# A chunked attention recurrence before two expert layers: other shapes for its small matmuls, one product for two uses, and a fixed order of the first transfers

## The chip, the cores and the metric

The kernel runs on one core of a Trainium2 chip. Its engines work from queues of their own: TensorE (PE for the matmuls, PEld for the loads of their weights), VectorE (DVE), ScalarE (ACT), GpSimd (POOL), and SyncE (SP), which issues nearly all DMAs here. The metric is the time of one execution on the device in microseconds (us), as the median of several. The profiled execution gives the rows.

## The reference

Three stages follow each other. The change is in the first and in the router of the second.

```python
# attention: B, H, S, D = 4, 8, 768, 40; the state is D x D for each (batch, head)
for t in range(S):
    y[:, :, t] = einsum('bhd,bhde->bhe', r_t, state)
    Sa = einsum('bhde,bhe->bhd', state, a_t)
    state = state * w_t[:, :, None, :] - einsum('bhd,bhe->bhde', Sa, b_t) + einsum('bhd,bhe->bhde', v_t, k_t)
x = y as (3072 tokens, 320)
# experts: skip = x @ w_skip > 0; the expert is argmax(x @ w_gate) of 8
x[skip] += gate * (relu(x @ w1[e]) @ w2[e])        # 320 -> 1024 -> 320
# dense layer, 320 -> 2048 -> 320
h = x @ w_in;  out = (h * sigmoid(1.702 * h)) @ w_out
```

## The kernel before, in words

The 768 steps are cut into 12 chunks of 64; all 32 (batch, head) pairs of a chunk are worked on together, packed in halves of 64 partitions. Everything in the recurrence is fp32, and an fp32 matmul stands as two instructions in the trace (a transpose as one).

For a chunk, `g_load` brings the decays (`wt`), the a vectors (`at`) and the k and b vectors (`kbT`). `g_prep` forms running products of the decays with two scans on VectorE (L216, L229) and their inverses. `g_a` (L265) and `g_kb` (L279) scale `at` and `kbT` by them on GpSimd; `g_f` and `g_kb` turn tiles with PE transposes (L251, L292). Three products of keys and a vectors follow. `g_gram` takes the 32-wide diagonal blocks that must be inverted (L320: 64 small matmuls for a chunk, with weights of 32 columns). `g_ag`, once for each of two parities, takes the whole 64 x 64 product (L378: 32 matmuls with 64x64 weights), which VectorE masks into `m0`, `m1` (L383). For each pair of chunks, VectorE inverts the blocks: a transpose (L330), 62 operations that depend on each other (L343, L346), a transpose back (L351), and DMAs from `Tc` into `tz` (L360), four for a chunk.

The serial part of a chunk is `g_chain`: sums X (L422 from the values, L427 from the state), the inverse times X (L444), a correction (L453), the inverse again, copies to `vu`. `g_state` (L483, L487) and `g_sn` (L509) make the next state. `g_vt`, `g_pq` (L554) and `g_post` (L578, L582) form the output rows, 64 matmuls on the keys and the state for a chunk, and `put` and `logits` (L827, L837) store them and form the router's sums with fp32 transposes and matmuls.

Between the products stand warm matmuls (L601) that compute nothing of use and keep TensorE active: `g_burst` adds 18 twice in a chunk, and `g_warm` adds more whenever the counted activity falls behind `PACE` times the elapsed time.

The order on every engine is fixed when the program is built. Each piece of work is a Python generator that yields what it needs and a cost, such as `'P1.05*.40'` (engine, us, counted activity); `weave` advances the one that can start first by these costs, and near-ties go by due times, the numbers in `RANK`. Each engine's queue then runs in that order, waiting on semaphores. SBUF of the later stages is opened when the last chunk is through its chain (`moves`).

Of the kernel before, what the change touches and what calls it, by code (L numbers as in the profile page):

```python
# [23 lines left out]
def host_attn(r, k, v, w, a, b):  # L24
    B, H_, S, D_ = r.shape
    NC = S // L

    def five(z):
        return z.reshape(2, 2, H, NC, L, D)

    k5, b5, v5, r5 = five(k), five(b), five(v), five(r)
    ch = lambda z: z.transpose(3, 0, 5, 2, 1, 4)
    kb = np.stack([ch(k5), ch(b5)], 5)
    kb[:, 1] = kb[:, 1, :, :, :, ::-1].copy()
    w5 = ch(five(w))
    wz = np.zeros((2, NC, 2, D, H, 2, L), np.float32)
    for h in (0, 32):
        wz[0][..., h + 1:h + 32] = w5[..., h:h + 31]
        wz[1][..., h:h + 31] = w5[..., h + 1:h + 32]
    pairs = lambda z: z.reshape(2, 2, H // 2, 2, NC, L, D).transpose(4, 3, 6, 0, 1, 2, 5).reshape(NC, 2, D, 1024)  # L40
    c = np.ascontiguousarray
    return dict(at=c(ch(five(a))).reshape(NC, 2, D, 1024), kbT=c(kb).reshape(NC, 2, D, 2048),
                rT=c(np.stack([pairs(r5), pairs(v5)], 3)).reshape(NC, 2, D, 2048),
                rv=np.pad(v5.transpose(3, 0, 4, 1, 2, 5), [(0, 0)] * 5 + [(0, 24)]).reshape(NC, 2, L, 1024), wt=c(wz.transpose(1, 2, 3, 0, 4, 5, 6)).reshape(NC, 2, D, 2048))
# [63 lines left out]
class Attn(Flow):  # L108
# [12 lines left out]
    EARLY = 'wt at0 at1 at2 kbT0 kbT1 W c_d1 c_d2 Za Z Tc tmp x y m0 m1 tz'.split()  # L121

    def __init__(self, tc, ctx, args, NC, emit_x):
# [14 lines left out]
        nc.vector.memset(self.wt, 1.0)  # L138
        for q, i in ((0, 0), (1, 31)):
            nc.vector.memset(self.wt[:, q].rearrange('p (a s) -> p a s', s=32)[:, :, i:i + 1], 0.0)  # L140
        for n, d in (('c_32', F32), ('c_16', F16)):
            shp = args[n].shape
            t = self.cst.tile([128, shp[1]], d, name=n)
            nc.sync.dma_start(out=t, in_=args[n])
# [6 lines left out]
        for n, i in (('c_d1', 0), ('c_d2', 31)):  # L151
            t = self.C[n] = new([128, 1024], F32, n)
            nc.gpsimd.memset(t, 0.0)
            nc.gpsimd.memset(t.rearrange('p (a s) -> p a s', s=32)[:, :, i:i + 1], 1.0)
        self.at = [new([128, 8, 2, 64], F32, f'at{i}') for i in range(3)]
        self.kbT = [new([128, 8, 2, 128], F32, f'kbT{i}') for i in range(2)]
        self.rT = [new([128, 2, 16, 64], F32, f'rT{i}') for i in range(2)]
        for t in self.at + self.kbT:
            nc.gpsimd.memset(t, 0.0)
        self.tz = new([128, 16, 64], F32, 'tz')  # L160
        self.tot = self.cst.tile([128, NC, 16, 2], F32, name='tots')
        self.scl = self.cst.tile([128, NC, 16], F32, name='scl')
        self.begin(self.SLOTS)
        self.ST = [new([128, 16, 64], F32, f'ST{i}') for i in range(2)]
        self.vu = [new([128, 32, 64], F32, f'vu{i}') for i in range(2)]
        for t in self.ST + self.vu:
            nc.gpsimd.memset(t, 0.0)
        self.S = self.tile([128, 8, 128], F32, 'S')
        nc.gpsimd.memset(self.S, 0.0)
        self.x, self.y = (self.tile([128, 664], F32, z) for z in 'xy')  # L170
        self.km = [self.tile([128, 1304], F32, f'km{i}') for i in range(self.KM)]
        for t in (self.x, self.y, *self.km):
            nc.gpsimd.memset(t[:, -24:], 0.0)
        self.zrow = self.ST[0][0:1].rearrange('p a b -> p (a b)')[:, :320].bitcast(F16)

# [6 lines left out]
    def g_zero(self):  # L182
        yield f'D1.1'
        self.nc.vector.memset(self.tz, 0.0)
        self.mark('zero', 0)

    def g_load(self, c):

        for n, need, t, cost in (('wt', ('W', c - 1), self.wt.rearrange('p a b -> p (a b)'), 1.6),
                                 ('at', ('X', c - 3), self.at[c % 3].rearrange('p a b c -> p (a b c)'), .8),  # L190
                                 ('kbT', ('km', c - 2), self.kbT[c % 2].rearrange('p a b c -> p (a b c)'), 1.6)):
            yield need
            if n == 'at':
                yield ('ag', c - 3)
            if n == 'kbT':
                yield ('ag', c - 2)
            for hb in range(2):
                yield f'Q.6>E{cost}'
                self.nc.sync.dma_start(out=t[64 * hb:64 * hb + 40], in_=self.args[n][c, hb])
            self.mark('l' + n, c)  # L200

    def g_prep(self, c):

        yield ('lwt', c)
        nc, s = self.nc, self.ch[c]
        wt = self.wt
        C1, C2 = self.C['c_d1'], self.C['c_d2']
        seg = lambda z: z.rearrange('p (a s) -> p a s', s=32)
        rv = slice(None, None, -1)
        yield ('F', c - 2)  # L210
        yield ('as', c - 2)
        yield ('kb', c - 2)
        yield 'D2.35'
        W = self.tile([128, 2, 1024], F32, 'W', 2)
        wf, wb = W[:, 0], W[:, 1]
        nc.vector.tensor_tensor_scan(out=wf, data0=wt[:, 0], data1=C1, initial=0.0, op0=ALU.mult, op1=ALU.add)  # L216
        yield 'D.2'
# [3 lines left out]
        yield 'D.36'  # L221
        tot = self.tile([128, 32, 1], F32, 'tot')
        nc.vector.reciprocal(out=tot, in_=full)
        yield 'D.15|G1.06'
        nc.vector.tensor_copy(out=seg(C2)[:, 1::2, 31:32], in_=tot[:, 1::2])
        f1 = seg(wf)[:, 0::2]
        nc.gpsimd.tensor_tensor(out=f1, in0=f1, in1=tot[:, 0::2].to_broadcast([128, 16, 32]), op=ALU.mult)
        yield 'D2.35'
# [3 lines left out]
        if c:  # L232
            yield 'D.5'
            nc.vector.tensor_tensor(out=self.scl[:, c - 1].rearrange('p (r h) -> p h r', r=2),
                                    in0=self.tot[:, c - 1, :, 1].rearrange('p (h r) -> p h r', r=2),
                                    in1=self.tot[:, c, :, 0].rearrange('p (h r) -> p h r', r=2), op=ALU.mult)
            self.mark('scl', c - 1)

    def g_f(self, c):

        yield ('W', c)
        nc, s = self.nc, self.ch[c]
        yield ('xo', 2 * c - 7)
        F = self.tile([128, 2, 8, 40], F32, 'F', 4)
        for q in range(2):
            yield '+g'
            sg = self.got
            yield 'P.45*.23'
            ps = self.pst(sg)
            for h in range(4):  # L250
                nc.tensor.transpose(out=ps[:, 128 * h:128 * h + 128], in_=s['W'][:, 0, 512 * q + 128 * h:512 * q + 128 * h + 128], identity=self.C['c_id'])  # L251
# [7 lines left out]
    def g_a(self, c):  # L259
# [5 lines left out]
        self.nc.gpsimd.tensor_tensor(out=t, in0=t, in1=self.ch[c]['W'][:, 0], op=ALU.mult)  # L265
        self.mark('as', c)

    def g_kb(self, c):
# [4 lines left out]
        W = s['W'][:, 1].rearrange('p (a b t) -> p a b t', b=2, t=64)  # L273
        kbT = self.kbT[c % 2]
        for q in range(2):
            yield 'G2.4'
            t = kbT[:, 4 * q:4 * q + 4].rearrange('p a b (e t) -> p (a b) e t', e=2)
            w = W[:, 4 * q:4 * q + 4].rearrange('p a b t -> p (a b) t').unsqueeze(2).to_broadcast([128, 8, 2, 64])
            nc.gpsimd.tensor_tensor(out=t, in0=t, in1=w, op=ALU.mult)  # L279
        self.mark('kb', c)  # L280
        yield ('Y', c - self.KM)
        km = self.km[c % self.KM]
        s['km'] = km
        km = km[:, :1280].rearrange('p (b q h d) -> p b q h d', b=2, q=2, d=40)
        for q in range(2):
            for par in range(2):
                yield '+g'
                sg = self.got
                yield 'P.45*.23'
# [9 lines left out]
    def g_gram(self, c0):  # L299
# [3 lines left out]
        yield ('zt', c0 - 2)  # L303
        Za = self.tile([128, 2, 2, 256], F32, 'Za')
        for i, c in enumerate(pair):
            yield ('as', c)
            yield ('kb', c)
            at, kbT = self.at[c % 3], self.kbT[c % 2]
            yield '+g2'
            sg = self.got  # L310
            yield 'P1.2*.41'
            Ad = [self.pst(z) for z in sg]
            for h in range(8):
                for par in range(2):
                    for half in range(2):
                        q = 64 * par + 32 * half
                        for hb in range(2):
                            r = slice(64 * hb, 64 * hb + 64)
                            o = 64 - 64 * hb + 32 * half
                            mm(Ad[hb][q:q + 32, 32 * h:32 * h + 32], lhsT=kbT[r, h, par, o:o + 32],  # L320
                               rhs=at[r, h, par, 32 * half:32 * half + 32], start=True, stop=True)
            self.mark('Ad', c)
            for hb in range(2):
                yield 'A.37'
                nc.scalar.copy(out=Za[:, i, hb], in_=Ad[hb][:, :256])
                self.give(sg[hb])
# [6 lines left out]
        yield 'P.43*.49'  # L333
# [14 lines left out]
        yield ('te', c0 - 3)  # L348
        Tc = self.tile([128, 2, 512], F32, 'Tc', 2)
# [5 lines left out]
        for i, c in enumerate(pair):  # L355
            yield ('U', c - 1)
            yield 'Q2.4>E1.2'
            for q in range(4):
                sl = slice(32 * q, 32 * q + 32)
                nc.sync.dma_start(out=tz[sl, :, q % 2 * 32:q % 2 * 32 + 32], in_=Tc[sl, i].rearrange('p (u t) -> p u t', t=32))  # L360
            self.mark('te', c)

    def g_ag(self, c, par):

        yield ('Ad', c)
        nc, s = self.nc, self.ch[c]
        at, kbT = self.at[c % 3], self.kbT[c % 2]
        yield ('B', c - 2)
        yield '+g2'
        sg = self.got  # L370
        yield 'P1.05*.54'
        ps = [self.pst(z) for z in sg]
        for h in range(8):
            for q in range(2):
                for hb in range(2):
                    r = slice(64 * hb, 64 * hb + 64)
# [3 lines left out]
        m = s[f'm{par}'] = self.tile([128, 2, 8, 64], F32, f'm{par}', 2)  # L380
        for hb in range(2):
            yield 'D.69'
# [1145 lines left out]
```

## Time and profile before

| | |
|---|---|
| median of 3 runs | 1057.68 us (1053.57 to 1057.70) |
| the profiled execution | 1056.17 us, of which 1054.3 us lie between the first and the last instruction |
| TensorE busy, matmuls / weight loads | 899.8 us / 700.3 us |
| VectorE, ScalarE, GpSimd busy | 575.9, 357.2, 372.6 us |
| mean granted TensorE clock | 0.923 of full |

Three stretches are told apart below by the time from the first instruction. Up to 114 us the first pair of chunks is loaded and inverted, until its first product with the inverse starts. The twelve chains then run to 515 us, and from there the expert stage runs to 705 us and the dense layer to the end. An engine that is busy is not therefore the bound; matmuls overlap, and the durations of PE rows are modelled, so that the time that a train of them takes is read from the chain of work.

### The profile page before, as it was taken

The page shows a single profiled execution, that of the slowest core. Times are in us where ns is not written, and L with a number is a line of the kernel's source. Part 1 is how long each engine was busy: PE and PEld are TensorE (multiplying, and loading weights), DVE is VectorE, ACT ScalarE, POOL GpSimd, SP SyncE. Part 2 cuts the span into 40 slices and gives each one's busy share as a digit, 9 for nine tenths or more (in the row PEclk, how much of TensorE's full clock was granted, in tenths as well). Part 3 has the DMA queues.
Part 4 walks back from the last instruction along what each step waited for, and adds up shares of the span by engine and source line. Part 5 has one row for each costly group of instructions (what it writes and reads, how often), then busy time and mean ns, then how long its engine had stood idle before and what let it go on. Part 6 is the DMA issues. An engine that isn't in the chain of part 4 may idle for free.

```text
span 1054.3 us, 36252 instructions
## 1 busy us (share of the span) xinstructions
PE 899.8 (85%) x16428; PEld 700.3 (66%) x16428; DVE 575.9 (55%) x1080; ACT 357.2 (34%) x708; POOL 372.6 (35%) x283
## 2 busy tenths in 40 slices
PE   5778798979998898899921889868799999999998
PEld 5768677879888788788811768753345555555565
DVE  2449577458768577383475888676972222122110
ACT  0110231323242233233344556634543333333330
POOL 5460312413532332411225367443543333333220
PEclk9889798989999999899855989988999999999999
DMA  5531243433344234123357976714301010100000
GB/s 128 137 86 28 47 119 74 112 100 105 96 119 111 69 116 121 34 73 74 114 176 227 256 206 201 247 31 123 85 27 39 13 38 13 39 14 13 13 20 28
DMA packets 81959, 96.86 MB, mean 92 GB/s; under 512 B 58740, under 2 KB 68728, under 8 KB 76856
## 3 DMA queue, kind: packets, MB, share of 16 engines
q1 hardware_dynamic: 79496, 90.12, 31.0%
q0 software_dynamic: 2304, 4.36, 1.5%
q8 instruction: 131, 2.15, 0.9%
q14 instruction: 28, 0.23, 0.1%
HBM read 70.70 MB, written 14.48 MB: 81 GB/s over the span
## 4 chain that ended last, share of the span: by engine, by line
PE 61%; DVE 13%; issue 11%; DMA 7%; ACT 3%; POOL 2%; SPq 2%; DVEq 0%; ACTq 0%; POOLq 0%
PE gx L601 8%; PE g L1352 5%; PE c L1392 5%; PE c L1393 5%; PE c L1391 5%; PE g L1354 3%; PE g L578 3%; PE g L444 3%; PE gx L1352 2%; PE g L554 2%; PE g L378 2%; PE g L487 2%; PE g L292 2%; PE g L483 1%; DMA kbT<-kbT 1%
## 5 line engine op out<-in xcount | busy, mean ns | idle before, releaser
L1374 POOL TENSOR_TENSOR glo<-g,ghi 128x512 f16<-128x512 f32 x96 | 114.8, 1198 | 200.3 <-ACT ghi L1373 200.1
L601 PE MATMUL gx<-c 128*128 128x128 f16 x2073 | 147.6, 227 | 11.8 <-issue 4.5
L601 PEld LDWEIGHTS <-c 128*128 128x128 f16 x2073 | 130.7, 102 | 19.1 <-issue 9.4
L1370 DVE SCALAR_TENSOR_TENSOR g<-g,sg 128x512 f32<-128x512 f32 x64 | 43.9, 688 | 135.9 <-ACT sg L1368 135.9
L1392 PE MATMUL c<-wo_lo,ghi 128*128 128x320 f16 x384 | 114.8, 299 | 1.9 <-DVE wo_lo L1299 1.9
L1391 PE MATMUL c<-wo_hi,ghi 128*128 128x320 f16 x384 | 114.8, 299 | 0.7 <-ACT wo_hi L1296 0.7
L1393 PE MATMUL c<-wo_hi,glo 128*128 128x320 f16 x384 | 115.0, 299 | 0.0
L1352 PE MATMUL g<-xt,wi_hi 128*128 128x512 f16 x320 | 81.7, 387 | 18.6 <-DMA xt<-xe 12.7
L1352 PEld LDWEIGHTS <-wi_hi 128*128 128x128 f16 x480 | 47.5, 99 | 65.3 <-DMA xt<-xe 13.0
L1373 ACT CAST ghi<-g 128x512 f16<-128x512 f32 x96 | 59.2, 618 | 79.3 <-DVE g L1370 78.5
L805 POOL TENSOR_TENSOR xr<-xo,xr 128x256 f16<-128x256 f32 (+1 forms) x44 | 21.2, 502 | 169.4 <-ACT xr L801 169.3
L279 POOL TENSOR_TENSOR kbT<-kbT,W 128x1024 f32<-128x1024 f32 x24 | 60.8, 2553 | 40.3 <-DMA kbT<-kbT 37.8
L343 DVE TENSOR_TENSOR tmp<-tm,Z 128x31 f32<-128x31 f32 (+15 forms) x186 | 63.3, 340 | 9.9 <-PE tm L336 4.1
L346 DVE TENSOR_TENSOR tm<-tm,tmp 128x31 f32<-128x31 f32 (+15 forms) x186 | 64.8, 349 | 5.9
L1368 ACT ACTIVATE sg<-g 128x512 f32<-128x512 f32 x64 | 37.8, 595 | 66.6 <-PE g L1354 66.6
L383 DVE TENSOR_TENSOR m<-g,c 128x512 f32<-128x512 f32 x48 | 31.1, 681 | 51.7 <-PE g L378 51.7
L1370 DVE SCALAR_TENSOR_TENSOR g<-gx,sg 128x512 f32<-128x512 f32 x32 | 22.1, 689 | 63.7 <-ACT sg L1368 63.4
L1038 POOL TENSOR_TENSOR w2l<-w2s,w2h 128x1280 f16<-128x1280 f32 x16 | 44.9, 2813 | 28.5 <-ACT w2h L1036 26.8
L1103 PE MATMUL g<-g_xt,w1h 128*128 128x240 f16 x220 | 31.5, 275 | 25.5 <-DMA g_xt<-g_x 25.4
L1354 PE MATMUL g<-xt,wi_lo 128*128 128x512 f16 x192 | 53.1, 386 | 0.0
L1392 PEld LDWEIGHTS <-ghi 128*128 128x128 f16 x384 | 37.6, 98 | 21.6 <-issue 1.0
L1354 PEld LDWEIGHTS <-wi_lo 128*128 128x128 f16 x288 | 28.5, 99 | 34.9 <-issue 1.6
(170 smaller groups left out, 1902.5 us busy)
## 6 DMA issues: line engine op xcount, KB each, us to landing
w2s<-w SPq DMA_DIRECT2D x8, 1280.0 KB
w1s<-w1a SPq DMA_DIRECT2D x8, 1024.0 KB
wt<-wt SPq DMA_DIRECT2D x24, 320.0 KB
rT<-rT SPq DMA_DIRECT2D x24, 320.0 KB
kbT<-kbT SPq DMA_DIRECT2D x24, 320.0 KB
vu<-rv SPq DMA_DIRECT2D x24, 256.0 KB
d_s<-wo SPq DMA_DIRECT2D x10, 512.0 KB
d_s<-wia SPq DMA_DIRECT2D x8, 512.0 KB
```

The costliest lines, as they stand in the source:

```text
L279: nc.gpsimd.tensor_tensor(out=t, in0=t, in1=w, op=ALU.mult)
L343: nc.vector.tensor_tensor(out=tv, in0=Tm[:, st:, st:st + 1].to_broadcast([128, n, st]), in1=Z[:, st:st + 1, 0:st].to_broadcast([128, n, st ...
L346: nc.vector.tensor_tensor(out=Tm[:, st:, 0:st], in0=Tm[:, st:, 0:st], in1=tv, op=ALU.subtract)
L601: self.nc.tensor.matmul(self.X[:, 384:], lhsT=self.C['c_i'], rhs=self.C['c_tm'][:, :128], start=self.first, stop=True, skip_group_check=True)
L1352: nc.tensor.matmul(h, lhsT=self.whi[:, k % 3, fs], rhs=xt[:, k], start=k == 0, stop=False)
L1354: nc.tensor.matmul(h, lhsT=self.wlo[:, k, fs], rhs=xt[:, k], start=False, stop=k == 2)
L1370: nc.vector.scalar_tensor_tensor(out=g, in0=h, scalar=2.0 ** -6, in1=sg2, op0=ALU.mult, op1=ALU.mult)
L1373: nc.scalar.copy(out=ghi[:, f], in_=g)
L1374: nc.gpsimd.tensor_tensor(out=glo[:, f], in0=g, in1=ghi[:, f], op=ALU.subtract)
L1391: nc.tensor.matmul(o, lhsT=ghi[:, f, s], rhs=self.ohi[:, f], start=f == 0, stop=False)
L1392: nc.tensor.matmul(o, lhsT=ghi[:, f, s], rhs=self.olo[:, f], start=False, stop=False)
L1393: nc.tensor.matmul(o, lhsT=glo[:, f, s], rhs=self.ohi[:, f], start=False, stop=f == 15)
```

## The change

Part by part, in the order of the diff (cut; the table `RANK` has new numbers throughout, and the costs that the pieces yield are new too):

- Loads: decays come once, unshifted, into `w5`, and ScalarE makes the two shifted copies (`g_split`). Transfers have 48 rows for each half in place of 40. The memsets become pieces of work (`sets`), and a counter `iss` fixes the order of the first transfers: wt, at, identity, kbT of chunk 0; wt, at, kbT of chunk 1; values; the rest. Constants of the router come after.
- `g_prep`: the reciprocal is split in two, the product of totals goes to GpSimd. For the first two chunks `kbT` is scaled on VectorE.
- The small product of `g_gram` goes. `g_ag` takes 16 matmuls with 64x128 weights for a parity, and both the mask (VectorE) and the diagonal blocks (eight ScalarE copies for a chunk) are read from its result.
- `tz` is filled by eight DMAs for a chunk. The inverse times X streams 40 columns in place of 64, as does the product that makes the state. The first chunk's products with the zero state go.
- `S` holds two heads block-diagonally; `g_post` runs for each half: 16 matmuls with the keys (40 columns) and 8 with the state (80 columns), in place of 32 and 32 for both halves.
- Router sums: 5 fp16 transposes and 8 fp16 matmuls on the high and low halves, in place of 3 and 3 in fp32.
- Warm matmuls: `PACE` .45 in place of .6 (.6 until the first chain), in groups of 6; the activity that the pieces are counted with is mostly larger. `weave` counts TensorE instructions and allows 3.75 us for each 128.

```diff
+        yield 'D', .97, ('z5', 0), lambda: D(self.w5, 1.0)
...
+        i = dict(wt=(1, 5), at=(2, 6), kbT=(4, 7))[n][c] if c < 2 else 10
+        if i > 1:
+            yield ('iss', i - 1)
+        yield f'Q.4>E{cost}|Q.4>E{cost}'
+        for hb in range(2):
+            self.nc.sync.dma_start(out=t[64 * hb:64 * hb + 48], in_=self.args[n][c, hb])
...
+        for q in range(2):
+            yield 'A1.1'
+            self.nc.scalar.copy(out=seg(self.wt[:, q])[:, :, 1 - q:32 - q], in_=seg(self.w5)[:, :, q:q + 31])
...
-            yield 'G2.4'
+            yield 'G2.4' if c > 1 else 'D1.15'
...
-                            mm(Ad[hb][q:q + 32, 32 * h:32 * h + 32], lhsT=kbT[r, h, par, o:o + 32],
-                               rhs=at[r, h, par, 32 * half:32 * half + 32], start=True, stop=True)
...
-        yield ('te', c0 - 3)
-        Tc = self.tile([128, 2, 512], F32, 'Tc', 2)
+        yield ('te', c0 - 1)
+        Tc = self.tile([128, 2, 512], F32, 'Tc')
...
-        yield ('B', c - 2)
+        yield ('zt', c - c % 2 - 2)
+        yield ('B', c - 3)
...
-        yield 'P1.05*.54'
+        yield 'P1.9*1.05*e*32'
         ps = [self.pst(z) for z in sg]
         for h in range(8):
-            for q in range(2):
-                for hb in range(2):
-                    r = slice(64 * hb, 64 * hb + 64)
-                    o = slice(64 * (q ^ hb), 64 * (q ^ hb) + 64)
-                    nc.tensor.matmul(ps[hb][o, 64 * h:64 * h + 64], lhsT=kbT[r, h, par, o], rhs=at[r, h, par], start=True, stop=True)
+            for hb in range(2):
+                r = slice(64 * hb, 64 * hb + 64)
+                nc.tensor.matmul(ps[hb][:, 64 * h:64 * h + 64], lhsT=kbT[r, h, par], rhs=at[r, h, par], start=True, stop=True)
...
+            for half in range(2):
+                o = 64 - 64 * hb + 32 * half
+                nc.scalar.copy(out=Za[o:o + 32, c % 2, par].rearrange('p (h t) -> p h t', t=32), in_=p3[o:o + 32, :, 32 * half:32 * half + 32])
...
-                mm(U[par][u, 64 * h:64 * h + 64], lhsT=tz[o, 8 * hb + h], rhs=x[o, 320 * hb + 40 * h:320 * hb + 40 * h + 64], start=h == 0, stop=True, **kw)
+                mm(U[par][u, 40 * h:40 * h + 40], lhsT=tz[o, 8 * hb + h], rhs=x[o, 320 * hb + 40 * h:320 * hb + 40 * h + 40], start=True, stop=True)
...
-                    mm(ps[64 * hb:64 * hb + 40, 64 * h:64 * h + 64], lhsT=km[:, p], rhs=vu[:, p], start=False, stop=True, **kw)
+                    mm(ps[64 * hb:64 * hb + 40, 64 * h:64 * h + 40], lhsT=km[:, p], rhs=vu[:, p, :40], start=False, stop=True, **kw)
...
+        for j in range(4):
+            for e in range(2):
+                for par in range(2):
+                    mm(Y[64 * par:64 * par + 64, 80 * j + 40 * e:80 * j + 40 * e + 40], lhsT=pq[:, 4 * par + j, e], rhs=km[:, hb, par, 2 * j + e],
+                       start=j + e == 0, stop=not c, **kw)
...
+            for j in range(4):
+                for par in range(2):
+                    mm(Y[64 * par:64 * par + 64, 80 * j:80 * j + 80], lhsT=rT[:, 8 * hb + 4 * par + j],
+                       rhs=S[:, 4 * par + j, hb].rearrange('p e d -> p (e d)'), start=False, stop=True, **kw)
...
-    PACE, SURPLUS = .6, .1
+    PACE, SURPLUS, FIRST = .45, .3, .6
...
+                    while page + n >= PAGE:
+                        t, cost, n, page = max(t + cost * (PAGE - page) / n, came), cost - cost * (PAGE - page) / n, n - (PAGE - page), 0
+                        came = t + FETCH
...
-            nc.tensor.transpose(out=ps[:n, 128 * k:128 * k + 128], in_=x[:, 128 * k:128 * k + n], identity=A.C['c_id'])
+            nc.tensor.transpose(out=p16[:, 128 * k:128 * k + 128], in_=xr[:, 128 * k:128 * k + 128], identity=A.C['c_i'])
```

## Rows read from the trace of the kernel before

**Rows 1.** Busy us (count) of PE, PEld, DVE, ACT, POOL; clock, DMA share, GB/s.

```profile
0.00:30.00 30.00, 15.88 (x219) 15.65 (x220) 9.00 (x9) 1.71 (x2) 15.94 (x24) 0.87 0.59 128
...
110.00:515.00 405.00, 366.46 (x11637) 328.49 (x11639) 256.03 (x547) 118.82 (x318) 121.14 (x97) 0.94 0.34 89
```

**Rows 2.** Chain of waits, shares by line: 0 to 110, then 110 to 515.

```profile
by line: issue 34.9%; DMA kbT<-kbT 14.1%; DMA wt<-wt 7.8%; POOL kbT L279 7.0%; DVE W L229 4.9%; PE g L378 3.3%; POOL vu L167 3.2%; POOL kbT L159 3.2%; POOL at L159 2.4%; DVE W L216 2.1%; SPq L782 1.8%; SPq L199 1.8%; POOL c_d L153 1.7%; POO
...
by line: PE gx L601 19.5%; issue 9.3%; PE g L578 7.3%; PE g L444 7.1%; PE g L554 6.0%; PE g L487 5.6%; PE g L378 4.9%; PE g L292 4.0%; PE g L483 3.8%; PE g L582 3.3%; PE g L320 3.3%; PE g L837 3.3%; PE gx L453 3.3%; PE gx L427 3.2%; PE gx L
```

**Rows 3.** Timeline up to the first product with the inverse: start, us, what.

```profile
14.90 0.51 SPq L199 DMA_DIRECT2D wt<-wt  x1
23.62 2.29 DVE L216 TENSOR_TENSOR_SCAN W<-wt,c_d 128x1024 f32<-128x1024 f32 x1 [19.33 <-DMA wt<-wt]
43.70 5.32 POOL L279 TENSOR_TENSOR kbT<-kbT,W 128x1024 f32<-128x1024 f32 x2 [1.28 <-DMA kbT<-kbT]
73.47 2.00 DVE L330 STREAM_TRANSPOSE Z<-Za 128x1024 f32<-128x1024 f32 x1 [6.05 <-ACT Za L325]
105.50 1.87 DVE L351 STREAM_TRANSPOSE Tc<-tm 128x1024 f32<-128x1024 f32 x1
107.39 2.77 SPq L360 DMA_DIRECT2D tz<-Tc  x4
114.17 1.99 PE L444 MATMUL g<-x,tz 64*64 64x64 f32 x64
```

**Rows 4.** Groups of VectorE instructions, 110 to 515 us.

```profile
L343 DVE TENSOR_TENSOR tmp<-tm,Z 128x31 f32<-128x31 f32 (+15 forms) x155 | 52.7, 340 | 6.9 <-PE tm L336 2.1
L383 DVE TENSOR_TENSOR m<-g,c 128x512 f32<-128x512 f32 x40 | 25.9, 681 | 40.5 <-PE g L378 40.5
```

**Rows 5.** Chain of work, pieces between 178 and 262 us: start, us, what.

```profile
180.97 2.12 PE gx L601 x36
...
185.25 0.72 PE g L837 x6
185.96 1.09 PE g L378 x64
187.05 0.48 PE g L827 x3
...
207.31 1.02 PE g L487 x32
...
234.07 0.64 PE g L530 x16
...
244.72 2.02 PE g L578 x64
246.74 1.09 PE g L582 x64
...
255.64 1.22 PE g L320 x79
```

**Rows 6.** Timeline of PEld around one stop, 168 to 174 us.

```profile
168.59 1.03 PEld L320 LDWEIGHTS g<-at,kbT 64*32 64x32 f32 x110
173.23 0.28 PEld L320 LDWEIGHTS g<-at,kbT 64*32 64x32 f32 x18 [3.60 <-issue]
```

**Rows 7.** Instruction queue: 170.4 to 172.4 us, 110 to 515, 346.5 to 361.

```profile
q8 instruction: 1, 0.02, 3.7%
...
q8 instruction: 91, 1.49, 1.6%
...
q8 instruction: 5, 0.08, 2.3%
```

**Rows 8.** Busy time: dense stretch, two stops; L601 alone, 110 to 515.

```profile
346.50:361.00 14.50, 12.49 (x546) 10.65 (x545) 6.18 (x10) 5.25 (x14) 4.93 (x3) 1.00 0.23 47
...
211.00:219.00 8.00, 3.45 (x145) 3.11 (x132) 3.96 (x3) 1.30 (x4) 0.00 (x0) 0.79 0.45 117
...
110.00:515.00 405.00, 95.14 (x1293) 80.25 (x1292) 0.94 0.34 89
```

More of the change, by code (lines that the diff above doesn't have):

```diff
@@ L137, in __init__ @@
         self.wt = new([128, 2, 1024], F32, 'wt')
-        nc.vector.memset(self.wt, 1.0)
-        for q, i in ((0, 0), (1, 31)):
-            nc.vector.memset(self.wt[:, q].rearrange('p (a s) -> p a s', s=32)[:, :, i:i + 1], 0.0)
+        self.w5 = new([128, 1024], F32, 'w5')
+        self.cin = []
         for n, d in (('c_32', F32), ('c_16', F16)):
@@ L176, in tile, with g_set, g_const @@
+    def g_set(self, eng, cost, what, fn):
+        yield f'{eng}{cost}'
+        fn()
+        self.mark(*what)
+    def g_const(self, i):
+        n, t = self.cin[i]
+        yield ('iss', 2 if i == 0 else 8)
+        yield 'Q.4>E1.0' if i == 0 else 'Q.4>E1.8'
+        self.nc.sync.dma_start(out=t, in_=self.args[n])
+        self.mark(n, 0)
+        self.note('iss', 3 if i == 0 else 9)
     def tile(self, shape, dt, name, bufs=1):
@@ L302, in g_gram @@
         pair = range(c0, c0 + 2)
[L303 to L317, printed above, removed]
-                            r = slice(64 * hb, 64 * hb + 64)
-                            o = 64 - 64 * hb + 32 * half
-                            mm(Ad[hb][q:q + 32, 32 * h:32 * h + 32], lhsT=kbT[r, h, par, o:o + 32],
-                               rhs=at[r, h, par, 32 * half:32 * half + 32], start=True, stop=True)
[L322 to L326, printed above, removed]
+        for c in pair:
+            yield ('ag', c)
+        Za = self.zas[c0 // 2]
         yield ('elim', c0 - 2)
@@ L356, in g_gram @@
             yield ('U', c - 1)
[L357 to L360, printed above, removed]
+            yield 'Q3.2>E1.2'
+            for q in range(8):
+                hb, half, par = 1 - q // 4, q // 2 % 2, q % 2
+                sl, o = slice(32 * (q // 2), 32 * (q // 2) + 32), 64 * par + 32 * half
+                nc.sync.dma_start(out=tz[o:o + 32, 8 * hb:8 * hb + 8, 32 * half:32 * half + 32],
+                                  in_=Tc[sl, i, 256 * par:256 * par + 256].rearrange('p (u t) -> p u t', t=32))
@@ new lines, in g_ag @@
+        if c // 2 not in self.zas:
+            self.zas[c // 2] = self.tile([128, 2, 2, 256], F32, 'Za')
+        Za = self.zas[c // 2]
+        m = s[f'm{par}'] = self.tile([128, 2, 8, 64], F32, f'm{par}', 3)
+        for hb in range(2):
+            yield 'D.69|A.36|A.36'
+            p3 = ps[hb].rearrange('p (h t) -> p h t', t=64)
+            nc.vector.tensor_tensor(out=m[:, hb], in0=p3, in1=self.two[:, hb:hb + 1].to_broadcast([128, 8, 64]), op=ALU.mult)
+            for half in range(2):
+                o = 64 - 64 * hb + 32 * half
+                nc.scalar.copy(out=Za[o:o + 32, c % 2, par].rearrange('p (h t) -> p h t', t=32), in_=p3[o:o + 32, :, 32 * half:32 * half + 32])
+            self.give(sg[hb])
@@ L408, in g_chain @@
         yield ('gram', c)
+        yield ('warm', 0)
         yield ('v', c)
         yield ('zero', 0)
+        yield ('zx', 0)
+        yield ('zs', 0)
         yield ('D', c - 1)
@@ L612, in g_warm @@
     def g_warm(self):
+        yield ('c_16', 0)
         yield 'Z1'
```

392 lines of the change are left out of this document (214 added, 178 removed), and 50 rows, old and new, of the table RANK.

## The prediction, made before the changed kernel ran

> **What bounds the kernel now.** I read the busy time by stretch first [rows 1]. From 110 to 515 us TensorE is the busiest engine (weight loads 328 of 405 us, VectorE 256). The change touches the two later stages, after 515 us, through the order of work alone. The chain of waits tells the two early stretches apart [rows 2]: up to 110 us it holds transfers, memsets, GpSimd and a long "issue" piece, while from 110 to 515 us nearly all of it is PE lines and PE's own "issue" (9.3%, 38 us). So in the chains PE's queue is the bound, and the largest single line in it, L601 (19.5%), computes nothing of use.
>
> The timeline of the start shows what is late [rows 3]: the second half of the first decays is issued only at 14.90 us, behind transfers that are not needed yet in SP's fixed order, and the scan starts at 23.62. The keys of chunk 0 are scaled at 43.70, the pair's blocks come to VectorE at 73.47, the inverse leaves at 105.50, and its first product starts at 114.17.
>
> The "issue" pieces come at fixed counts. In one of them PE stops after 110 of 128 small matmuls for 3.60 us [rows 6], and in that pause one packet of about 16 KB arrives on the instruction queue [rows 7]. In the chains 91 such packets go with 11,639 weight loads, one for each 128. Where PE runs densest, five packets and 545 matmuls take 14.5 us [rows 7, 8], some 3.4 us for 128, an estimate of the least time for a packet. A train of 64 that takes 1.09 us, or of 128 in 1.2 us [rows 5, 6], uses them up faster. I read this as PE waiting for its own instructions.
>
> The Trainium skill says otherwise: "Runtime: NRT & Kernel Launch", section "Instruction fetch mechanics", has PE stream its program ahead, with fetch hidden. The trace [rows 6, 7] does not bear this out; it is a rival below.
>
> **The change, part by part.** The profiled execution took 1056.17 us, 1.5 us under the median, with 1.9 us outside its span; I sum against it.
>
> *Start.* The values no longer stand ahead of the decays, decays are half the bytes, and the memset in front of them is half as long. Walking the new order: decays issued at 2 us; the old wait to landing was 8.5 us in traffic (14.90 to the scan), now 6 to 8.5, so 9; the new ScalarE copies cost about 1 us each, of which one stands in front; scans and small operations 5.5 us (2.29 for each scan), so W of chunk 0 at 16. Scaling kbT on VectorE is at 0.68 us for 512 columns [rows 4] some 2.7 us, against 5.32 on GpSimd. Chunk 1 follows with 5.5 us of scans to 22 to 24; its keys are the seventh transfer: about 3.3 MB up to there, at the 128 GB/s of the first 30 us 26 us plus 2. So keys scaled at 31, product and copies 5 (up to 9 at half clock), transpose 2: elimination starts at 38 to 42. It took 105.50 - 75.47 = 30 us with masks and a scan between its steps; the 62 operations alone are 21 us at L343's 340 ns [rows 4]. I take 28. Then 2 for the transpose back; the DMAs, eight for four, cost 2.8 us (same bytes) to 5.5 (twice the issues) and landing and x another 4. U of chunk 0 starts at about 74 in place of 114: -40 us. Bounds: -20 (transfers twice as slow, all of the masks between the steps), -50 (26 us of elimination, landing without queues).
>
> *Chains: warm matmuls.* L601 has 1293 instructions [rows 8], 59 ns each (36 in 2.12 us [rows 5]), 76 us. The bursts, 36 a chunk, stay: 24 us. The other 52 us are paced. The activity that the pieces state sums to 12 us a chunk before and 20 after, and the pace falls from .6 to .45 of the time. At some 30 us a chunk the products alone are then above the pace, and warm matmuls come only where PE would idle. I take two thirds away, -35 us; bounds 0 and -52.
>
> *Chains: stops for instructions.* Without L601 a chunk has 968 PE instructions: 8 + 16 transposes, 128 + 128 in the gram, 320 in the chain, 68 + 8 for the state, 16, 128 and 128 for the output, 18 in the router, 2 for the inverse's start. After it is 750: the gram is 64, output products 96 in place of 128, the router 26. With 35 us of L601 gone, 11,639 becomes some 8,550, 67 packets, at least 228 us in place of 309. The 38 us of stops shrink as the average distance of packets grows from 4.4 to over 5 us: -24 us, bounds 0 and -38.
>
> *Chains: the products themselves*, per chunk [rows 5]. Router sums: 2 x (0.48 + 0.72) = 2.4 us become 26 fp16 instructions, at L601's 59 ns 1.5 us: -0.9. State: 2 x 1.02 us with 40 columns in place of 64, between no gain and 40/64: -0.4. Output: 2.02 + 1.09 us; the keys' part keeps 64 instructions and weights of 64 columns, the state's part has 32 with 80 columns, at the 32 ns of L578 1.0 to 1.3: -0.1. Gram: L320 1.2 and L378 2 x 1.09, together 3.4 us, become 64 instructions with 64x128 weights. No row has this as an fp32 product; L530 has the same shape as a transpose, 40 ns (16 in 0.64), and on full height products (L837, 120 ns) stand one tenth above what transposes take, so 45 ns or 2.9 us, -0.5; bounds 34 ns (twice L378's 17) and 60 (half of L837, the two halves overlapping). The inverse times X is held by its 64 weight columns: nothing. Sum -1.9, for 11.5 chunks -22 us; bounds -4 and -48.
>
> *What is given back.* PE's terms make -81 us. VectorE has 256 us of work in 401; at 320 it would be 80% busy, and elimination, masks and the serial chain of a chunk are next in line. I let a quarter return: -61, so 340 us from the first U to the last. At a third 347; at 285 (VectorE nine tenths busy) the floor, -116.
>
> *Costed at nothing.* ScalarE gets some 5 us a chunk (shifted copies, eight block copies, four for S): 119 us busy in 405 leave room, and decays are prepared a chunk ahead; where that cover is gone, the two copies would put 2 us into each chunk's preparation. SP gets six more issues a chunk; the DMAs into `tz` stand ahead of the loads of the next chunks, and for the chain they run beside the state's products, 5 to 8 us either way. GpSimd's added product is a quarter microsecond. Tc has one buffer for two: it waits for DMAs that are a pair old. The later stages keep their operations: 0, with 15 us either way for the new order.
>
> Sum: 1056 - 40 - 61 = **955 us**.
>
> **Rivals.** *The clock falls.* PE was granted 0.94 in the chains [rows 1], held up by L601; with less of it and unchanged idle stretches the clock may go to its lower level more often. PE's work is (405 - 38) x 0.94 = 345 us at full clock, 345 - 57 = 288 after. At 0.75 that is 384 us and 14 of stops: 398, no gain in the chains, 1014 in all. Below 0.68 (288/0.68 + 14 = 438) the start's gain is lost too and the kernel is **slower**; at 0.6, 494 us, 1110. For it: the clock follows what PE does, 0.79 in 8 us with two stops against 1.00 in the densest stretch [rows 8]. Against it: the stops themselves become fewer, and paced matmuls still fill idle time. Chance .12, of which .05 slower.
>
> *PE's relief turns into waits.* In-order queues wait for masks, inverses or buffers as soon as PE is early; only 15 us stay of 61: 1001. VectorE's idle time (L383 waits 40 us for PE [rows 4]) speaks against it. Chance .15.
>
> *The stops are not fetches.* Then they do not follow the count of instructions, the 24 us do not come (18 after the quarter), and the time is 973. The packet in the pause and the one packet for each 128 speak against it; that a train of 64 often runs on without a stop speaks for it. Chance .07. This is how the page named above would have it.
>
> *The first transfers stay late*, behind each other at the early rate, and the start gives only 15: 980. Chance .12.
>
> *Nearly all arrives*: start -48, chains -95: 913. Chance .12.
>
> **How the numbers follow.** The forecast has .42, with 930 to 980 as its own range. From the cases, 915 to 1010 holds eight in ten: below lies half of the best case, above the fallen clock. Faster by over 0.5% (5 us, about what a measurement of this kernel can tell from none): .93; within: .02; slower: .05.
>
> **What would show it.** First product with the inverse at 70 to 80 us, elimination from 40 on. L601 under 900 instructions in all of the chains; 65 to 72 instruction packets there; "issue" under 5% of their chain of waits. L378's successor at 45 ns an instruction; over 55 the gram costs more than before. Granted clock at 0.9 or more between first and last U, 340 us apart. Wrong would be: a clock under 0.8, waits of PE on VectorE in place of "issue", or a first U after 95 us.

## The result, and the profile after

The changed kernel takes 1006.99 us (median of four, 1001.9 to 1017.3), the kernel before 1057.69 in the same runs. Without its longest execution, which ran at a lower clock, the ratio is 0.9511, with an interval of 0.9456 to 0.9567. It is faster, by 51 us and not by the 101 of the forecast (1056 to 955).

The profile is of that longest one, so most rows below are from a second run of the same kernel beside the experiments (the profiled execution took 1013.37 us, its span 1011.5; ratio 0.9547, 0.9485 to 0.961). Over both runs its executions lie between 1001.9 and 1022.2 us; the lengths of parts are read from the profiles.

The three parts, from the first and last instruction of U's line (L444 before, L492 after):

```
                     span    first U   first to last U   after it
before             1054.3     114.2        401.4          538.7
after              1015.4      89.2        378.9          547.3
after, second run  1011.5      82.0        382.6          547.0
forecast                        74          340          no change
```

Busy time by stretch, the second run, with the columns of [rows 1]:

```profile
0.00:30.00 30.00, 12.82 (x90) 11.86 (x91) 21.01 (x22) 8.50 (x15) 22.99 (x29) 0.85 0.75 168
82.00:465.00 383.00, 338.62 (x9322) 305.64 (x9321) 244.15 (x535) 160.59 (x389) 120.92 (x107) 0.95 0.47 96
```

2,300 instructions have left PE's queue, yet PE is still 88% busy (338.6 of 383; 366.5 of 405 in [rows 1], 90%), the clock is where it was, and VectorE has no more to do. ScalarE rose from 119 to 161 us.

The start, its timeline (answers to [rows 3]):

```profile
8.41 2.29 DVE L256 TENSOR_TENSOR_SCAN Wf<-wt,c_d 128x1024 f32<-128x1024 f32 x1 [0.76 <-POOL c_d L169]
...
14.24 2.52 DVE L323 TENSOR_TENSOR kbT<-kbT,Wb 128x1024 f32<-128x1024 f32 x2 [0.54 <-DMA kbT<-kbT]
...
39.63 1.98 DVE L353 STREAM_TRANSPOSE Z<-Za 128x1024 f32<-128x1024 f32 x1 [0.96 <-ACT Za L417]
...
72.55 1.95 DVE L375 STREAM_TRANSPOSE Tc<-tm 128x1024 f32<-128x1024 f32 x1
74.52 5.27 SPq L385 DMA_DIRECT2D tz<-Tc  x8
...
81.99 1.16 PE L492 MATMUL g<-x,tz 64*64 64x40 f32 x64
```

The scan comes at 8.4 us and not 23.6, the pair's blocks at 39.6 and not 73.5. From there to the first U it takes 42.4 us; before it was 40.7, so all of the gain of the start lies ahead of the inverse.

The chains: groups of instructions from 82 to 465 us (answers to [rows 4], and the warm and gram lines), and the instruction queue there [rows 7]:

```profile
L648 PEld LDWEIGHTS <-c 128*128 128x128 f16 x1086 | 70.5, 103 | 11.1 <-issue 8.1
L367 DVE TENSOR_TENSOR tmp<-tm,Z 128x31 f32<-128x31 f32 (+15 forms) x155 | 52.7, 340 | 8.0 <-PE tm L360 3.3
L406 PEld LDWEIGHTS g<-at,kbT 64*128 64x128 f32 x576 | 34.0, 188 | 1.9 <-issue 0.4
L417 ACT COPY Za<-g 32x256 f32<-32x256 f32 x72 | 26.1, 363 | 33.6 <-DVE m L414 32.8
L414 DVE TENSOR_TENSOR m<-g,c 128x512 f32<-128x512 f32 x36 | 23.7, 678 | 17.8 <-PE g L406 17.8
```

```profile
q8 instruction: 73, 1.20, 1.5%
```

The warm line has 1,086 instructions, forecast under 900. The gram runs at 34.0 us / 576 = 59 ns an instruction, forecast 45. Packets fell from 91 to 73 (65 to 72 forecast). The block copies (L417) were idle for 33.6 us in front, 32.8 of them for the mask (L414): both read the same PSUM bank, and the first copy of a pair carries a wait for VectorE. In the costs that the order was built from, `'D.69|A.36|A.36'`, mask and copies stand side by side.

The chain of waits by line, 120 to 456 us (answers to the second line of [rows 2]):

```profile
by line: PE gx L648 14.2%; issue 9.7%; PE g L406 8.1%; PE g L603 6.4%; PE g L627 5.9%; PE g L492 5.8%; PE g L536 3.8%; PE g L336 3.8%; PE g L531 3.7%; PE gx L501 3.4%; PE gx L469 3.2%; PE gx L475 3.1%; PE g L634 3.0%; ACT vu L509 2.4%; PE g
```

Adding up the pieces of these chains by engine shows the change that matters (before: 123 to 505 us; shares of the length of the pieces):

```
                           PE products   PE warm   issue   ScalarE   rest
before                       67.6%        18.9%     9.5%    0.7%     3.3%
after, second run            58.9%        14.2%     9.5%    9.0%     8.4%
the same without paced warm  58.9%         6.8%     8.8%    9.3%    16.2%
```

Before, 96% of the path was PE's queue; after, it is 83%. Applied to 401 and 383 us, PE's products lost some 46 us on it, warm products 22 and stops 2, and ScalarE's copies and the rest gained some 50. A stretch of the chain after, without pieces under 0.05 us:

```profile
199.65 1.98 PE g L406 x32
201.63 0.68 DVE m L414
202.34 0.36 ACT Za L417
202.71 0.36 ACT Za L417
203.10 0.42 ACT vu L509
...
216.56 1.21 PE gx L475 x63
...
218.15 4.24 DMA at<-at
222.46 0.08 issue
222.59 2.33 POOL at L309
224.91 2.92 POOL xr L877 x2
```

The values `vu`, which the next state needs, wait in ScalarE's queue behind block copies, which wait for a mask. Then a load that came late holds GpSimd, and PE behind it.

### The profile page after: what moved, and what is told of

Same layout as the page of the kernel before. It is cut to its first block, busy times and chain, and to the rows that moved or that the text cites. A ratio compares the mean times of both kernels' runs of the same rounds, so it can differ in the third digit from the quotient of the medians.

```text
span 1015.4 us, 29929 instructions
## 1 busy us (share of the span) xinstructions
PE 856.8 (84%) x13149; PEld 660.1 (65%) x13149; DVE 577.3 (57%) x1076; ACT 415.4 (41%) x803; POOL 356.2 (35%) x291
## 4 chain that ended last, share of the span: by engine, by line
PE 28%; DVE 9%; issue 7%; DMA 6%; POOL 2%; ACT 2%; SPq 1%; POOLq 0%; DVEq 0%; ACTq 0%
PE g L1423 5%; PE c L1463 5%; PE c L1464 5%; PE c L1462 5%; PE g L1425 3%; PE gx L1423 3%; DMA w2s<-w 2%; DMA g_x<-xd,g_ig 2%; PE gx L1425 1%; DVE g L1441 1%; DVE d_k L1341 1%; POOL w2l L1109 1%; DMA tab<-c_pair,r_si 1%; DVE e_xo L1227 1%; PE g L1174 1%
## 5 line engine op out<-in xcount | busy, mean ns | idle before, releaser
L648 PE MATMUL gx<-c 128*128 128x128 f16 x1482 | 111.1, 232 | 6.8 <-issue 3.7
L648 PEld LDWEIGHTS <-c 128*128 128x128 f16 x1482 | 97.3, 104 | 13.2 <-issue 9.7
L323 POOL TENSOR_TENSOR kbT<-kbT,Wb 128x1024 f32<-128x1024 f32 x20 | 46.9, 2361 | 44.9 <-DMA kbT<-kbT 21.9
L406 PE MATMUL g<-at,kbT 64*128 64x64 f32 x768 | 57.5, 305 | 5.5 <-POOL at L309 4.8
L406 PEld LDWEIGHTS g<-at,kbT 64*128 64x128 f32 x768 | 54.0, 216 | 8.9 <-POOL at L309 5.6
L417 ACT COPY Za<-g 32x256 f32<-32x256 f32 x96 | 34.8, 363 | 45.9 <-DVE m L414 44.8
L269 POOL TENSOR_TENSOR Wf<-Wf,tot 128x512 f32<-128x512 f32 x12 | 21.7, 1811 | 88.2 <-DVE tot L267 70.0
```

Source lines behind the costliest of these rows:

```text
L406: nc.tensor.matmul(ps[hb][:, 64 * h:64 * h + 64], lhsT=kbT[r, h, par], rhs=at[r, h, par], start=True, stop=True)
L648: self.nc.tensor.matmul(self.X[:, 384:], lhsT=self.C['c_i'], rhs=self.C['c_tm'][:, :128], start=self.first, stop=True, skip_group_check=True)
```

## The experiments

Ratios are to the kernel before on the same chip. "The same order" means that every other instruction keeps its place. The first four expectations have theory letters of their own: there A says that PE's queue is the bound and the warm products stand in its way, and B that PE waits for other engines and warm products only fill those waits. In the later ones: A, banks held longer by the gram delay the second pass of U (x ready to that U: 83 us in twelve chunks, 47 before); B, PE's own work and its stops; C, VectorE; D, PE's order and VectorE together; F, an order made for shorter durations.

**The changed kernel again** (a0_same). 

> The changed kernel as it is, for a profile beside the others and for the spread of its time. Both theories: 1000 to 1010 us, first product with the inverse near 89 us, the last one near 455 to 470 us.

Measured: 0.9547 (0.9485 to 0.961), the yardstick for what follows.

**No paced warm products** (no_paced), the same order.

```diff
-                self.warm(6)
+                if ('U', 0) not in self.done:
+                    self.warm(6)
```

> Leaves out the paced warm matmuls after the first chain (about 750 of 1482; the bursts stay); every other instruction keeps its place. Theory A (PE's queue is the bound and warm matmuls stand in its way, as the forecast had it): some 50 us of PE time leave the chains, 965 to 980 us. Theory B (the order leaves PE waiting for evacuations and the warm matmuls only fill those waits): within 8 us of the changed kernel, or slower by 10 to 40 us if the granted clock falls below 0.85 between 90 and 470 us.

Measured: 0.9502 (0.9418 to 0.9586), not to be told from 0.9547, as B had it. Busy time from first to last U:

```profile
88.00:456.00 368.00, 315.53 (x8655) 279.31 (x8654) 242.13 (x535) 159.44 (x388) 118.16 (x106) 0.91 0.47 98
```

654 of the 1,482 warm products are gone (the expectation said some 750), 45 us of PE's time. The granted clock goes from 0.95 to 0.91, the other products take 262 us in place of 247 (summed from the start of one weight load to the next, without idle time), and idle time grows from 60 to 76. In this profile the chains last 368 us, 11 to 15 less than in the two of the changed kernel, so at most a third of the 45 us came back, and the times do not confirm that much. What warm products held on the path, transfers, GpSimd and VectorE now hold (the table above).

**The kernel before without its paced warm products** (before_no_paced), the same edit there. 

> The kernel before without its paced warm matmuls after the first chain, all else in place. This is the forecast's largest term by itself (52 us of paced matmuls in the chains). Theory A: 1010 to 1025 us. Theory B: 1050 to 1060, or slower if the clock falls (above 1070 with a granted clock under 0.85 in the chains).

Measured: 0.9744 (0.9692 to 0.9795), some 27 us faster, between A and B: of the 57 us of warm products that went, about half came back. Its five executions lie between 1035.6 and 1061.6 us, though, and the one with a profile (1054.44) still needs 403 us from first to last U, for 401. So it is not shown in which part of the kernel the others gained.

**The gram with 64x64 weights** (narrow_gram), the same order.

```diff
-            for hb in range(2):
-                nc.tensor.matmul(ps[hb][:, ...], lhsT=kbT[r, h, par], ...)
+            for q in range(2):
+                for hb in range(2):
+                    o = slice(64 * (q ^ hb), 64 * (q ^ hb) + 64)
+                    nc.tensor.matmul(ps[hb][o, ...], lhsT=kbT[r, h, par, o], ...)
```

> The gram's full product with 64x64 weights (64 instructions for a parity at some 17 ns in place of 32 at some 67), in the same places of the order; the result is the same. Theory A (PE bound): 1.0 us less for a parity, 24 parities, less half an instruction packet more for each chunk: 985 to 995 us. Theory B (two of four PSUM banks are held by mask and block copies whatever the product takes): 995 to 1005 us. If the stops for instructions were the bound, 25 more packets would make it slower, 1015 to 1025 us.

Measured: 0.961 (0.9555 to 0.9666), 1023.99 us for 1013.62 on the same chip; the two intervals overlap a little. Its gram and its chain of waits:

```profile
L408 PEld LDWEIGHTS g<-at,kbT 64*64 64x64 f32 x1152 | 20.2, 138 | 9.3 <-issue 7.6 <-ACT Za L419 0.5
```

```profile
by line: issue 13.6%; PE gx L650 12.8%; PE g L494 6.9%; PE g L408 4.5%; PE g L605 4.4%; PE g L629 4.2%; DVE tm L370 3.5%; PE gx L503 3.4%; DVE tmp L367 3.4%; PE gx L471 3.2%; PE g L336 2.9%; SPq L385 2.9%; PE g L538 2.9%; PE g L533 2.4%; DM
```

At 17.5 ns an instruction its gram is busy 14 us less than the wide one in the chains, and the kernel is not faster but some 10 us slower: 576 more instructions, four more packets, "issue" from 9.7 to 13.6%. That is what the expectation has for stops as the bound.

**Trains of one shape** (trains), by themselves. 

> No part of the reference: eight trains of 384 products each on TensorE, of the shapes of this kernel, with 64 warm products between them. If PE's instructions come in pages of 128 products that take at least 3.4 us each, a train of small products cannot run under 27 ns a product over its whole length, whatever it costs within a page: the fp32 64x64 train runs at 17 ns within a page (as short runs of it do in the kernel) and 27 to 30 ns over all; if the instructions are fetched far enough ahead to be hidden, at 17 ns throughout. The gram's fp32 64x128 train: 45 ns by the forecast, 65 to 70 ns by the row of the changed kernel.

The timeline of PE (every fp32 product shows as two instructions, so the "128 products" of the expectation are 128 instructions), and the instruction queue over the whole run:

```profile
65.28 2.09 PE L42 MATMUL g<-x,w 64*64 64x64 f32 x128 [1.36 <-issue]
69.00 2.09 PE L42 MATMUL g<-x,w 64*64 64x64 f32 x128 [1.64 <-issue]
72.73 2.09 PE L42 MATMUL g<-x,w 64*64 64x64 f32 x128 [1.64 <-issue]
...
81.85 43.09 PE L45 MATMUL g<-x,w 64*128 64x64 f32 x768
...
128.55 158.96 PE L48 MATMUL g<-x,w 64*128 64x64 f32 x768
```

```profile
q8 instruction: 53, 0.87, 0.7%
```

After the first 259, the small products run 128 at a time and then stop, once every 3.73 us, 29 ns an instruction over all. The wide ones (L45, the two row halves in turn) never stop and take 56 ns, between the 45 of the forecast and the 65 to 70 of the expectation. None of the other trains stops either; the fastest two take 29.4 ns an instruction. The 53 packets are one for each 128 of the run's 6,784 instructions. I read this as PE waiting for its instructions, at 3.7 us for 128, which shows only where a shape is faster than 29 ns. The Trainium skill ("Runtime: NRT & Kernel Launch", section "Instruction fetch mechanics") has instructions refilled in blocks of 16 KiB, as here, and calls the fetch hidden; this train does not bear the second out.

**The chain keeps its two banks** (hold_banks).

```diff
-            yield '+g2'
-            sg = self.got
+            if not i:
+                yield '+g2'
+                sg = self.got
...
-                self.give(sg[par])
```

> The changed kernel, in which the chain keeps its two PSUM banks from the first pass of U to the second instead of giving them back and asking for two again; the order is planned anew. Theory A (the gain of the chains went into a wait that the change itself brought: the second pass of U comes 83 us later over the twelve chunks than its inputs allow, against 47 before, because the gram and the output products hold the four shared banks): that wait falls under 45 us, and the time from the first to the last instruction of U falls from 379 to 383 us to 350 to 365; 985 to 1000 us in all. Theory B (PE's own work and the stops for its instructions set the pace, and a U that comes earlier only moves what stands in front of it): the wait falls but is found again in other places, 370 to 390 us from first to last U, 1000 to 1020 us.

Measured: 1.0016 (0.9956 to 1.0076), 408 us from first to last U. The wait before the second pass of U falls from 83 to 59 us, not under 45, and VectorE waits longer for the gram (17.8 us in the second run):

```profile
DVE m L414 <- PE g L406: 67.5, 16, 18.1
```

Either theory expected a shorter time. The order was made anew, so this edit does not tell the banks from the order.

**No block copies after the first pair** (no_block_copies), the same order.

```diff
-            self.zas[c // 2] = self.tile([128, 2, 2, 256], F32, 'Za')
+            self.zas[c // 2] = self.tile([128, 2, 2, 256], F32, 'Za') if c < 2 else self.zas[0]
...
-            for half in range(2):
+            for half in range(2 if c < 2 else 0):
```

> The changed kernel in the same order without the 80 ScalarE copies that lift the diagonal blocks out of the gram for chunks 2 to 11 (the inverse of the first pair of chunks is then computed again for the later ones). Each bank of the gram is given back after the mask, some 0.74 us earlier, and ScalarE has 29 us less to do. Theory A: 8 to 20 us faster than the changed kernel, and the wait before the second pass of U shorter by as much. Theory B: within 5 us of it.

Measured: 0.9542 (0.948 to 0.9603), as the changed kernel and as B had it; the wait before the second pass of U is 80 us for 83. Neither the 0.74 us a bank of theory A nor ScalarE's 29 us hold the stage by themselves.

**The elimination's product twice** (more_elim), the same order.

```diff
             nc.vector.tensor_tensor(out=tv, ..., op=ALU.mult)
+            if c0:
+                nc.vector.tensor_tensor(out=tv, ..., op=ALU.mult)
```

> The changed kernel in the same order, with the product of every elimination step issued twice for the last five pairs of chunks (the second writes the same numbers): 155 more VectorE instructions at 0.34 us, some 50 us of VectorE work. Theory C (VectorE sets the pace of the chains): 40 to 50 us slower than the changed kernel. Theories A and B: VectorE is busy 247 us of 379 and has room; 0 to 20 us slower, from waits of the gram's masks behind it.

Measured: 0.9992 (0.9936 to 1.0047), some 47 us slower than the changed kernel by the ratios, for 54 us more of VectorE work. The elimination comes onto the path:

```profile
by line: issue 10.4%; DVE tmp L370 10.3%; DVE tmp L367 10.2%; DVE tm L373 9.6%; PE g L409 7.5%; PE gx L651 7.0%; PE g L630 3.0%; DVE pq L610 2.6%; DMA at<-at 2.4%; PE g L495 2.2%; PE g L336 2.1%; DVE Wf L256 2.0%; PE g L637 1.9%; DVE m L417
```

This looked like theory C, so the reverse was tried.

**Half of the elimination** (half_elim), the same order, **and without paced warm products as well** (half_elim_no_paced).

```diff
             yield d
+            if c0 and st % 2:
+                yield d
+                continue
             nc.vector.tensor_tensor(out=tv, ...)
```

> The changed kernel in the same order without every other step of the elimination for the last five pairs of chunks (their inverse is then not complete): 160 VectorE instructions, some 27 to 54 us of VectorE work, less, in five places. Theory C (VectorE alone paces the chains): 25 to 45 us faster than the changed kernel. Theory D (PE's order with its stops and VectorE's elimination are both near the limit, so that what is taken from one of them alone is met by the other): 3 to 15 us faster. Theory B (PE alone): within 3 us.

> As half_elim, and without the paced warm products after the first chain as well. Theory D: 25 to 45 us faster than the changed kernel, more than the two reliefs gave one by one (no_paced: none that could be measured). Theory C: as half_elim alone, within 5 us. Theory B: as no_paced alone, within 5 us, since what is left of PE's work and stops is the same.

Measured: 0.9568 (0.9504 to 0.9631) and 0.9503 (0.9423 to 0.9584). Busy time of the second, first to last U:

```profile
90.00:461.00 371.00, 315.71 (x8658) 278.46 (x8657) 193.71 (x375) 159.54 (x388) 120.26 (x108) 0.91 0.47 97
```

VectorE's work fell from 244 to 194 us, PE's by 45 of warm products, and nothing is gained over the changed kernel or over no_paced. C and D fall; what B expected of the two came true. In its chain of waits PE's products, stops and ScalarE's copies still have 75%; the rest has moved on to loads of `at` and `kbT`, GpSimd's scaling of them, VectorE's scans and SP's queue.

**The start** (start_fix), the same order.

```diff
+        if not c0:
+            Tm = ...; mm(Tm[...], lhsT=self.C['c_i'], ...)
         yield 'D1.95'
...
-                nc.sync.dma_start(out=tz[...], ...)
+                (nc.scalar if not c and q % 2 else nc.sync).dma_start(out=tz[...], ...)
```

> The changed kernel in the same order but for the first pair of chunks: the identity product that the first elimination works on is issued ahead of its warm products, and of the eight DMAs that bring the first inverse to its place four are issued by ScalarE's queue. If the 5.1 us wait for that product and the 5.3 us of DMA issue are what the first inverse lacks against the forecast, the first product with the inverse starts 5 to 8 us earlier than in the changed kernel (82 to 89 us), and the time falls by 4 to 9 us; if the start is held by something else, less than 3 us.

Measured: 0.9507 (0.9427 to 0.9586), no gain that the measurement can tell; first U at 86.5. The 5.1 us wait for the identity product that the first profile showed is 0.5 in the second run. From the end of the transpose back to the first U it is 7.5 us with two queues (79.0 to 86.5) and 7.5 with one in the second run (74.5 to 82.0). What stands there is the same in both. First the second run, then start_fix:

```profile
76.77 2.89 POOL L269 TENSOR_TENSOR Wf<-Wf,tot 128x512 f32<-128x512 f32 x1 [9.65 <-DVE tot L267]
...
79.71 0.66 PE L295 MATMUL g<-c,Wf 128*128 128x128 f32 x4 [0.63 <-POOL Wf L269]
...
81.08 0.44 ACT L484 ACTIVATE x<-gx 128x320 f32<-128x320 f32 x1 [2.31 <-PE gx L648]
...
81.56 0.49 PE L648 MATMUL gx<-c 128*128 128x128 f16 x6 [0.53 <-ACT x L484]
```

```profile
84.23 0.66 PE L295 MATMUL g<-c,Wf 128*128 128x128 f32 x4 [0.62 <-POOL Wf L269]
84.73 0.83 PE L653 MATMUL gx<-c 128*128 128x128 f16 x12
86.09 0.49 PE L653 MATMUL gx<-c 128*128 128x128 f16 x6 [0.53 <-ACT x L489]
86.51 1.16 PE L497 MATMUL g<-x,tz 64*64 64x40 f32 x64
```

In PE's queue, transposes that prepare chunk 2 (L295) stand ahead of the first U. They wait for GpSimd (L269), which waits for VectorE's small operations behind the masks; then come warm products, the second half of x, and U. In the chains of waits of both runs neither the issue nor the landing of the eight DMAs stands on this path, so their half of the edit could not help. In the profiles of the changed kernel and its variants the first U lies between 81.9 and 90.5 us.

**The order made anew with measured durations** (replanned).

```diff
-        yield 'P1.9*1.05*e*32'
+        yield 'P2.0*1.05*e*32'
...
-            yield 'D.69|A.36|A.36'
+            yield 'D.69>A.38>A.38'
...
-            yield 'P.96*.66*b*64'
+            yield 'P1.27*.66*b*64'
...
-            yield 'Q3.2>E1.2'
+            yield 'Q5.2>E1.2'
...
-RANK = [...]
+RANK = [...]
```

> The changed kernel with the same operations, whose order is made anew: the costs that the order is built from are set to the durations of the traces (64 products of X 1.24 us for 1.0, of U 1.27 for 0.96, of the output 1.17 and 0.77 for 0.93 and 0.55, of the state 0.77 for 0.62, six warm products 0.42 for 0.32, the gram's mask and its two block copies one after the other and not side by side, the inverse's eight DMAs 5.2 us for 3.2), and the priorities are searched again under these costs. Theory F (no single engine paces the chains: the order was made for shorter operations than the chip has, so in-order engines wait for each other in turn, and what one relief frees another wait takes): 350 to 368 us from first to last U for 379 to 383, 980 to 1000 us in all. Theory B (PE's own work and its stops for instructions pace the chains, in whatever order): 370 to 385 us, within 8 us of the changed kernel.

Measured: 0.9557 (0.9512 to 0.9603), 379 us from first to last U, as B had it. F falls too, for the one new order that was tried. No version here beats the changed kernel by more than its measurement can tell.

## Why the prediction was right in sign and half in size

*The range held by luck.* 1006.99 us lies 3 us inside the stated 915 to 1010, and outside the 930 to 980 of the forecast; the second run's 1013.62 lies above both. It is the terms that decide, and they came short: of the start's 40 us, 25 to 32 came, of the chains' 61 only 19 to 22, and the later stages took 8 back.

*The start: the mechanism right, its size off.* Elimination starts at 42.1 us in the second run (38 to 42 forecast). The first U was to follow at 74 and comes at 82 to 89. A part of that is the sum: its own terms (38 to 42, then 28, 2, 2.8 to 5.5, and 4) give 75 to 82. In the second run the steps with what lies between them take 30.5 us for 28, and the way from the transpose to U 7.5, where chunk 2's preparation ahead of U in PE's queue had no term (start_fix); a wait for the identity product adds up to 5 in the first profile.

*Chains, warm matmuls: the step that failed.* I took two thirds of the paced ones away for -35 us. 1,086 of 1,293 are still there [rows 8], -6 us of PE's time (82 to 76, summed from one weight load to the next). They stand where the counted activity falls behind, and PE was left as idle as before (60 us for 56); that the one explains the other is my reading. And a warm product was not worth its length: without the paced ones the changed kernel is no faster by its times (no_paced), and the kernel before gained some 27 us for 57 (before_no_paced).

*Chains, stops.* The trains bear the mechanism out and narrow_gram agrees with it. The packets came almost as forecast (73 for 65 to 72), but the time did not follow the count: "issue" has 36 us of the path for 38, not 24 less. The mean distance of packets grew to 5.2 us as forecast. The stops come mostly in the dense trains, which the change left dense, as the longest of PE's waits in the second run show:

```profile
PE g L603 <- issue: 7.6, 7, 2.5
PE g L492 <- issue: 6.1, 5, 2.4
PE gx L501 <- issue: 5.7, 3, 3.5
PE gx L475 <- issue: 4.3, 7, 1.6
```

These lines run at 17 to 20 ns an instruction, under the 29 that the supply sustains.

*Chains, products.* -22 forecast; their time, summed in the same way, fell from 263 to 247 us, -16. The gram is the term off: 59 to 67 ns for 45, 3.8 to 4.3 us a chunk for 2.9. "Over 55 the gram costs more than before" holds for its busy time; that the kernel would be faster with a shorter gram in more instructions, narrow_gram does not bear out.

*What is given back.* A quarter was to return; of what PE lost on the path (some 70 us), some 50 did. That is the rival "PE's relief turns into waits" (1001 us, chance .15), though on the path ScalarE's copies (9%), and loads, SP and GpSimd together (5%), have more than VectorE (3%), so the sign that I named for it did not show.

*What paces the chains now is open.* None of the reliefs that were tried makes the kernel faster by more than can be told: warm products, VectorE's elimination, both, the block copies, another order. More VectorE work costs nearly its length, and more PE instructions cost some 10 us by the medians, though the gram is busy for less. That fits a stage in which several paths across in-order queues are about equally long; it is what the runs leave, not shown by one of them. Theory B is a rival that is not excluded: what it expected came true in half_elim, half_elim_no_paced, no_block_copies and replanned, and failed in more_elim and hold_banks. PE's products and stops still have 68% of the path, and no run takes useful PE products away without adding instructions. The loads wait for buffers; a third `kbT` and a fourth `at` (12 KB a partition) were not tried.

*Clock.* 0.93 and 0.95 between first and last U in the two profiles, for 0.94 before: no fall. *Later stages.* +8 us, inside the 15 either way; not followed up.

## What to carry to other kernels

Before a filler is counted as a saving, take it out by itself: here 57 us of it were worth some 27 in the kernel before, and 45 us nothing that could be told in the changed one. Work that was free beside a path that is nine tenths one engine, such as ScalarE's copies here, can become part of the path once that engine is relieved. For dense trains of small products count instructions beside busy time: the form of the gram that was busy for less was not the faster one.

## What the runs showed of the hardware

- PE's instructions come at 3.73 us for 128 pairs of a weight load and a matmul, 29 ns a pair (trains); 64x64 fp32 pairs at 16 ns then stop once in each 128.
- fp32 weights of 64x128 run at 56 ns a pair with the two row halves in turn. On one half alone it is 207 ns over the train, with PE busy throughout. In that train the granted clock, at 1.00 in the train before it, went down to 0.50 (1.2 GHz), and it was 1.00 again in the train after it (128x64 weights). So the 207 ns hold both the form and the lower clock; this is one execution. The three trains, the one on one half in two stretches:

```profile
81.90:124.90 43.00, 43.00 (x770) 42.93 (x770) 0.00 (x0) 0.00 (x0) 1.00 0.01 2
128.60:140.00 11.40, 11.40 (x79) 11.40 (x78) 0.00 (x0) 0.00 (x0) 0.75 0.01 1
140.00:287.00 147.00, 147.00 (x691) 147.00 (x691) 0.00 (x0) 0.00 (x0) 0.50 0.00 1
293.00:315.00 22.00, 22.00 (x758) 22.00 (x758) 0.00 (x0) 0.00 (x0) 1.00 0.02 4
```
